# Half of the triangular inversions done 16 wide and merged by two small products, with a product and the mixture moved

## The chip, the cores and the metric

The kernel runs on one core of one Trainium2 chip. The time is the device time of one execution in microseconds (us); lower is better. TensorE is called PE in the profile (its weight loads PEld), VectorE DVE, ScalarE ACT, GpSimd POOL, and SyncE (which issues nearly all DMAs here) SP.

## The reference

A recurrence over 768 time steps runs for 4 batches of 8 heads with a 40 by 40 state, and its output goes through a gated mixture over the sequence:

```
for t in range(S):
    y[:, :, t] = einsum('bhd,bhde->bhe', r_t, state)
    Sa = einsum('bhde,bhe->bhd', state, a_t)
    state = state * w_t[:, :, None, :] - einsum('bhd,bhe->bhde', Sa, b_t) + einsum('bhd,bhe->bhde', v_t, k_t)
x = y, heads side by side                      # 768 x 320 for each batch
h = maximum(x @ w_in, 0); u, v = halves of h   # 512 columns each
v = (v - mean) / sqrt(var + 1e-6)              # over the 512 columns
v = einsum('ts,bsd->btd', w_spatial, v) + b_spatial[:, None]
out = (u * v) @ w_out
```

## The kernel before, in words

**The recurrence in chunks.** `phase1` cuts the time axis into chunks of 64 steps. Two batches are worked on together, so there are 24 chunk steps, numbered 0 to 23 below, 12 for each pair of batches. In a chunk the steps are solved at once by a lower triangular system with unit diagonal. Its inverse is needed. Each 64 by 64 triangle is cut into blocks of 32: the two diagonal blocks are inverted on DVE, and the block below them is made of products (`b_l21`, `b_zt`, `b_x21`).

**The inversion.** `lprime` (PE) and `lblock` (DVE) make the diagonal blocks of one chunk, tile `Lc`. For four chunks, a group, `invert` transposes them into `A` (DVE), does 30 substitution steps of two DVE instructions each (lines 351 and 355), and transposes the result into `XT0` and `X11` (lines 360 and 362). It runs as a generator: one step at a time is put among the other DVE work. Group 0 is done in one go at the start, since chunk 0 waits for it. Groups 1 to 5 are for chunks 4 to 7, 8 to 11 and so on.

**The step.** For chunk s, and two halves g of the heads, `c_bp` (PE) multiplies the carried state `Mc`, `c_bp_out` (ACT) evicts it, `c_ff` and `c_ff_out`, `c_xx` and `c_xx_out` follow in the same way, `c_mp` and `c_mp_out` (DVE, tiles `mn` and `Mc`) make the next state, `c_y` and `c_y_out` (DVE, tile `y`) the output. The products of chunk s+1 that don't need the state (`b_copy`, `b_lka`, `b_lka_out`, `b_tok`, `b_h` and so on) and the preparation of later chunks (`scan1`, `scan2`, `at_mul`, `sl_mul` on DVE) stand between them. `b_lka` is the masked product: its result is evicted by ACT into `At` and masked there by POOL (`strict`).

**The order.** Each function is put into a list with a time, `at(t, fn, ...)`, in units of chunk steps; the list is sorted, and the instructions of each engine stand in that order and run in it. The small products of phase 1 write tiles named `bk` from a pool of two PSUM buffers, so a product waits until the one two before it has been read.

**The mixture.** `decode` (DVE, ACT, POOL) turns `w_in` into two float32r parts, from step `T_DEC` on. The mixture's first product (`m_u`, four of each six slots, and `m_v`, two of six) has 72 slots, four for each chunk step, from step `T_MOE` on. What is left of them after chunk 23 runs in between the instructions of `phase2` (`spatial`, lines 173 to 178, and `proj`, line 193), which a scheduler puts in order. The loads of phase 2 for a batch, `vload`, take memory that the mixture's tiles hold until they are done.

## Time and profile before

| What | Value |
|---|---|
| Runs | 725.81 us median of 3 (721.95 to 728.2) |
| The profiled execution | 728.03 us, its span 726.2 us |
| Mean granted clock of TensorE | 0.901 |
| Busy share: PE, PEld, DVE, ACT, POOL | 82%, 74%, 62%, 57%, 40% |
| Chunk steps 0 to 22 | 29.8 to 524.9 us of the span |
| From chunk step 23 to the end | 524.9 to 726.2 us |

The busy shares are means over a span with three different parts: the start, the chunk steps without the mixture (0 to 10) and those with it (11 to 22), and the end, where phase 2 takes over. What bounds the time is read for each part by itself, by cutting the span at the first product of each `c_bp`.

### The profile page before, as it was taken

Reading aid. Unit: us, or ns where it says so; the run is one execution under the profiler, and the core shown is the slowest. Engines: PE = TensorE matmul, PEld = TensorE weight load, DVE = VectorE, ACT = ScalarE, POOL = GpSimd, SP = SyncE. Lnnn points to the kernel's source line nnn. Section 1 sums busy time; section 2 is a strip of 40 time slices with the busy share of each in tenths; the row PEclk is TensorE's granted clock in tenths of the full one; section 3 lists DMA queues with packets and bytes.
Section 4 is the critical chain, followed back from the end, with each engine's and each line's share of the span. In section 5 each row is a group of like instructions: output and inputs, shape, how many; then the busy total and the mean of one; then the engine's idle time right before and its main releaser. Section 6 shows DMA issues by size and latency. Waiting matters only on the chain. (4 is left out here: it accounts for less than half of the span.)

```text
span 726.2 us, 25447 instructions
## 1 busy us (share of the span) xinstructions
PE 592.8 (82%) x10784; PEld 535.0 (74%) x10784; DVE 448.6 (62%) x884; ACT 415.1 (57%) x904; POOL 289.7 (40%) x486
## 2 busy tenths in 40 slices
PE   2707776587776877989988999899999999599997
PEld 1606665586665776868877788788789998499997
DVE  7898689968999998758797565311247201343221
ACT  2406763377655666878878798798754423332112
POOL 4102230124433435354554543464549822373221
PEclk9956997578977888989999999999899999799999
DMA  9443675294444535454365344344263533650001
GB/s 186 86 90 69 104 145 112 51 185 94 106 91 101 112 82 118 112 126 112 102 187 165 85 133 127 106 120 116 73 198 108 158 108 100 189 180 34 28 28 55
DMA packets 101337, 81.35 MB, mean 112 GB/s; under 512 B 33576, under 2 KB 90152, under 8 KB 99304
## 3 DMA queue, kind: packets, MB, share of 16 engines
q1 hardware_dynamic: 100680, 78.01, 43.3%
q10 hardware_dynamic: 544, 1.72, 1.1%
q8 instruction: 85, 1.39, 0.9%
q14 instruction: 28, 0.23, 0.1%
HBM read 59.20 MB, written 20.50 MB: 110 GB/s over the span
## 5 line engine op out<-in xcount | busy, mean ns | idle before, releaser
L396 POOL TENSOR_SCALAR_AFFINE_SELECT Rt<-Rt 64x512 f32<-64x512 f32 (+1 forms) x144 | 84.1, 585 | 102.2 <-ACT Rt L582 74.4
L545 ACT ACTIVATE Rt<-bp 64x416 f32<-64x416 f32 x96 | 49.1, 512 | 68.2 <-PE bp L535 66.4
L351 DVE TENSOR_TENSOR itmp<-A 128x30 f32<-128x30 f32 (+9 forms) x180 | 73.7, 409 | 3.3
L396 POOL TENSOR_SCALAR_AFFINE_SELECT At<-At 64x512 f32<-64x512 f32 x48 | 36.9, 768 | 94.6 <-ACT At L406 92.5
L173 PE MATMUL pg<-wsh,vh 128*128 128x384 f32 x192 | 65.1, 339 | 0.0
L174 PE MATMUL pg<-wsl,vh 128*128 128x384 f32 x192 | 65.0, 339 | 0.0
L175 PE MATMUL pg<-wsh,vl 128*128 128x384 f32 x192 | 64.8, 337 | 0.0
L355 DVE TENSOR_TENSOR A<-A,itmp 128x30 f32<-128x30 f32 (+9 forms) x180 | 59.0, 328 | 6.2
L535 PE MATMUL bp<-lin,Mc 40*64 40x104 f32 x768 | 53.1, 301 | 11.1 <-DVE y L640 10.3
L535 PEld LDWEIGHTS bp<-lin,Mc 40*64 40x64 f32 x768 | 46.2, 167 | 16.0 <-DVE y L640 13.4
L177 DVE TENSOR_TENSOR g<-pg,bb 128x384 f32<-128x384 f32 x32 | 17.7, 553 | 63.9 <-PE pg L175 56.9
L702 DVE BATCH_NORM_STATS2 bs<-vr 128x6 f32<-128x512 f32 x24 | 16.6, 690 | 60.3 <-ACT vr L696 60.2
L54 POOL TENSOR_TENSOR gl<-g,gh 128x384 fp32r<-128x384 f32 x32 | 33.8, 1062 | 47.7 <-ACT gh L50 47.7
L582 ACT ACTIVATE Rt<-ch 64x416 f32<-64x416 f32 x96 | 49.2, 512 | 3.9 <-PE ch L571 1.5
L326 PE MATMUL bk<-at,sl 64*32 64x32 f32 x1536 | 24.4, 221 | 28.6 <-DVE sl L313 14.5
L553 PE MATMUL ch<-Rt,At 128*64 128x104 f32 x768 | 46.0, 277 | 1.2 <-issue 1.2
L50 ACT ACTIVATE gh<-g 128x384 fp32r<-128x384 f32 x32 | 16.7, 522 | 52.3 <-DVE g L178 52.3
L441 PE MATMUL bk<-ident,sl 128*128 128x128 f32 x192 | 31.7, 297 | 17.4 <-ACT tk L447 6.9
L553 PEld LDWEIGHTS ch<-Rt,At 128*64 128x64 f32 x768 | 40.3, 152 | 5.7 <-issue 3.0
L326 PEld LDWEIGHTS bk<-at,sl 64*32 64x32 f32 x1536 | 20.6, 132 | 30.7 <-DVE sl L313 14.6
L571 PE MATMUL ch<-ffs,xf 64*64 64x104 f32 x768 | 42.6, 263 | 0.0
L54 POOL TENSOR_TENSOR vl<-raw,vh 128x512 fp32r<-128x512 f32 x24 | 32.1, 1350 | 25.8 <-ACT vh L50 24.8
(121 smaller groups left out, 1604.2 us busy)
## 6 DMA issues: line engine op xcount, KB each, us to landing
ein<-in_early SPq DMA_DIRECT2D x40, 387.0 KB
lin<-in_late SPq DMA_DIRECT2D x48, 160.0 KB
uts<-ur SPq DMA_DIRECT2D x48, 128.0 KB
vns<-vr SPq DMA_DIRECT2D x24, 256.0 KB
raw<-vns SPq DMA_DIRECT2D x24, 256.0 KB
ut<-uts SPq DMA_DIRECT2D x24, 256.0 KB
Rt<-in_vtok SPq DMA_DIRECT2D x48, 80.0 KB
xs<-y SPq DMA_DIRECT2D x48, 80.0 KB
```

The lines of the kernel that those rows point to most:

```text
L54: eng.tensor_tensor(out=lo, in0=x, in1=hi.bitcast(F32), op=ALU.subtract)
L173: nc.tensor.matmul(pg, lhsT=vh[:, dc], rhs=w_h, start=(i == 0), stop=False)
L174: nc.tensor.matmul(pg, lhsT=vh[:, dc], rhs=w_l, start=False, stop=False)
L175: nc.tensor.matmul(pg, lhsT=vl[:, dc], rhs=w_h, start=False, stop=(i == NT - 1))
L326: nc.tensor.matmul(pl[o:o + HB, n, :], lhsT=sl[PR[par], n, par, cs], rhs=at[PR[par], n, cs], start=True, stop=True,)
L351: nc.vector.tensor_tensor(out=tp, in0=A[:, k + 1:, k:k + 1].broadcast_to([P, m, k]), in1=A[:, k:k + 1, 0:k].broadcast_to([P, m, k]), op=AL ...
L355: nc.vector.tensor_tensor(out=A[:, k + 1:, 0:k], in0=A[:, k + 1:, 0:k], in1=tp, op=ALU.add)
L396: nc.gpsimd.affine_select(out=t, in_=t, pattern=[[0, k], [1, C]], base=0, channel_multiplier=-1, compare_op=ALU.is_gt, fill=0.0,)
L535: nc.tensor.matmul(bp[PR[par], q, :], lhsT=Mc[RR[par], n, :], rhs=li[RR[par], n, C:], start=(q == 0), stop=False, skip_group_check=True,)
L545: nc.scalar.activation(Rt[par][PR[par], gp, :], st["bp", g][PR[par]], AF.Copy)
L553: nc.tensor.matmul(ff[PR[1 - par], q, :], lhsT=At[par][:, n, :], rhs=Rt[par][:, n, :], start=True, stop=True,)
L582: nc.scalar.activation(Rt[par][PR[par], gp], xx[PR[1 - par]], AF.Copy, scale=-1.0)
```

## The change

Four things are done. Groups 1 and 2 (chunks 4 to 11) are inverted by `invert16`: the two 16 wide diagonal blocks of each 32 wide block are inverted together, in 14 steps of two DVE instructions on both at once, after a second memset; the block below them comes from two products on PE for each chunk (`merge_z`, `merge_x`) with an ACT eviction between them and a DVE addition and a DVE transpose behind them. `Lc` gets three buffers. `b_copy`, `b_lka` and `b_lka_out` go behind `c_ff`, so that `At` needs one buffer for the chunk it serves, and `b_tok` comes to where they were. `T_DEC` goes from 4.2 to 3.2 and `T_MOE` from 11 to 10. `b_h_out` of chunk 0 is written ahead of the first inversion, which leaves its engines' order as it was.

```diff
+    QB = 16
+    QUAD = (1, 2)
...
-            st["Lc", s // GS] = inv.tile([P, GS * NU, HB], F32, name="Lc")
+            st["Lc", s // GS] = inv.tile([P, GS * NU, HB], F32, name="Lc", bufs=3)
...
+    def invert16(g):
+        Lc = st["Lc", g]
+        Af = inv.tile([P, HB * HB + HB], F32, name="A")
+        A = Af[:, 0:HB * HB].rearrange("p (t s) -> p t s", s=HB)
+        D = Af.rearrange("p (b x) -> p b x", b=2)[:, :, 0:HB * QB]
+        D = D.rearrange("p b (t s) -> p b t s", s=HB)[:, :, :, 0:QB]
+        nc.vector.transpose(out=A, in_=Lc.rearrange("p u t -> p t u"))
+        yield
+        nc.vector.memset(Af[:, 0:HB * HB:HB + 1], 1.0)
+        nc.vector.memset(A[:, QB:, 0:QB], 0.0)
+        for k in range(1, QB - 1):
+            m = QB - 1 - k
+            tp = ps_i.tile([P, 2, m, k], F32, name="itmp")
+            nc.vector.tensor_tensor(
+                out=tp, in0=D[:, :, k + 1:, k:k + 1].broadcast_to([P, 2, m, k]),
+                in1=D[:, :, k:k + 1, 0:k].broadcast_to([P, 2, m, k]), op=ALU.mult,
+            )
+            nc.vector.tensor_tensor(
+                out=D[:, :, k + 1:, 0:k], in0=D[:, :, k + 1:, 0:k], in1=tp, op=ALU.add
+            )
+            yield
...
+        nc.vector.transpose(out=X11.rearrange("p u t -> p t u"), in_=A.rearrange("p t s -> p s t"))
+        yield
+        nc.vector.transpose(out=XT0.rearrange("p u t -> p t u"), in_=A)
+        yield
+
+    def merge_z(s):
...
+        zp = ps_k.tile([P, NU, HB], F32, name="bk")
+        for n in range(NU):
+            for o in range(0, P, HB):
+                nc.tensor.matmul(
+                    zp[o:o + HB, n, :], lhsT=Lc[o:o + QB, u0 + n, :],
+                    rhs=X11[o:o + QB, u0 + n, :], start=True, stop=True,
+                )
+        z = Lc[:, u0:u0 + NU]
+        nc.scalar.activation(z, zp, AF.Copy)
...
+    def merge_x(s):
...
+        xp = ps_k.tile([P, NU, QB], F32, name="bk")
+        for n in range(NU):
+            for o in range(0, P, HB):
+                nc.tensor.matmul(
+                    xp[o:o + HB, n, :], lhsT=z[o:o + HB, n, :],
+                    rhs=XT0[o:o + HB, u0 + n, QB:], start=True, stop=True,
+                )
+        nc.vector.tensor_tensor(out=XT0[:, us, QB:], in0=xp, in1=XT0[:, us, QB:], op=ALU.add)
+        nc.vector.transpose(
+            out=X11[:, us].rearrange("p u t -> p (u t)"), in_=XT0[:, us].rearrange("p u t -> p (u t)")
+        )
...
-            at(b + 0.11 + 0.02 * par, b_copy, q, par)
-            at(b + 0.17 + 0.02 * par, b_lka_out, q, par)
+            at(b + 0.38 + 0.01 * par, b_copy, q, par)
+            at(b + 0.44 + 0.01 * par, b_lka_out, q, par)
...
-            at(b + 0.40 + 0.03 * par, b_tok, q, par)
-            at(b + 0.43 + 0.03 * par, b_tok_out, q, par)
-        at(b + 0.115, b_lka, q)
+            at(b + 0.12 + 0.03 * par, b_tok, q, par)
+            at(b + 0.14 + 0.03 * par, b_tok_out, q, par)
+        at(b + 0.40, b_lka, q)
...
+        b = GS * g - 1
+        if g in QUAD:
+            gen = invert16(g)
+            for k in range(QB - 1):
+                at(t0 + (b - 0.1 - t0) * k / (QB - 2), step, gen)
+            at(b + 0.02, step, gen)
+            at(b + 0.10, step, gen)
+            for j in range(GS):
+                at(b + j + 0.26, merge_z, GS * g + j)
+                at(b + j + 0.47, merge_x, GS * g + j)
+            continue
...
-    T_DEC, T_MOE = 4.2, 11
+    T_DEC, T_MOE = 3.2, 10
```

The order shows the change at three places. The first is DVE in chunk step 3, from the `y` of chunk 2 to the next state; there before stand 50 rows from `Lc` to the first `mn`, of which these are the first three and the last ten:

```order
L337 TENSOR_TENSOR Lc<-bk,maskl 128x256
L351 TENSOR_TENSOR itmp<-A 128x238
L355 TENSOR_TENSOR A<-A,itmp 128x17x14
...
L355 TENSOR_TENSOR A<-A,itmp 128x2x29
L351 TENSOR_TENSOR itmp<-A 128x30
L355 TENSOR_TENSOR A<-A,itmp 128x30
L281 SCALAR_TENSOR_TENSOR S<-ein_121,ends 128x528
L285 RECIPROCAL ends<-S 128x8
L360 STREAM_TRANSPOSE XT_1890<-A 128x32x32
L362 STREAM_TRANSPOSE X_1891<-A 128x32x32
L290 SCALAR_TENSOR_TENSOR Et<-ein_121,ends 128x528
L307 TENSOR_TENSOR at<-ein_121,Et 128x512
```

And now 20 rows stand there, of which these are the first twelve and one more (lines 396 and 398 are the transposes of `invert16`, 64 is the decoding, 428 is `merge_x`):

```order
L339 TENSOR_TENSOR Lc<-bk,maskl 128x256
L396 STREAM_TRANSPOSE X_1668<-A 128x32x32
L398 STREAM_TRANSPOSE XT_1667<-A 128x32x32
L283 SCALAR_TENSOR_TENSOR S<-ein_120,ends 128x528
L287 RECIPROCAL ends<-S 128x8
L292 SCALAR_TENSOR_TENSOR Et<-ein_120,ends 128x528
L309 TENSOR_TENSOR at<-ein_120,Et 128x512
L64 TENSOR_SCALAR d_t_1756<-d_raw 128x512
L315 TENSOR_TENSOR sl<-ein_120,S 128x1024
L339 TENSOR_TENSOR Lc<-bk,maskl 128x256
L69 TENSOR_SCALAR d_t_1757<-d_raw 128x512
L428 TENSOR_TENSOR XT_1667<-bk,XT_1667 128x8x16
```

The substitution has left chunk step 3 altogether (it ends in step 2), and the decoding and the merge have come in.

The second place is PE in chunk step 6, from `c_bp` to `c_xx`. Before, `b_lka` (line 389) stands between `c_bp` (535) and `c_ff` (553), and `b_tok` (441) and `b_l21` (458) between `c_ff` and `c_xx` (571):

```order
L535 MATMUL bp_2728<-lin_136,Mc 64x104 x8
L535 MATMUL bp_2746<-lin_136,Mc 64x104 x8
L389 MATMUL bk<-at,sl 64x64 x16
L553 MATMUL ch<-Rt_132,At_2424 64x104
...
L441 MATMUL bk<-ident,sl 128x128 x8
L458 MATMUL bk<-sl,at 32x32 x16
L571 MATMUL ch<-ffs,xf_130 64x104 x16
```

Now `b_tok` (508) and `merge_z` (408) stand ahead of `c_ff` (621), and `b_lka` (453) and `merge_x` (424) behind it:

```order
L602 MATMUL bp_2886<-lin_136,Mc 64x104 x8
L602 MATMUL bp_2904<-lin_136,Mc 64x104 x8
L508 MATMUL bk<-ident,sl 128x128 x8
L408 MATMUL bk<-X_1668,Lc 32x32 x32
L621 MATMUL ch<-Rt_132,At_2619 64x104
...
L453 MATMUL bk<-at,sl 64x64 x16
L424 MATMUL bk<-XT_1667,Lc 32x16 x32
L525 MATMUL bk<-sl,at 32x32 x16
L639 MATMUL ch<-ffs,xf_130 64x104 x16
```

The masked product and the transposes of `b_tok` have changed places, and 64 small matmuls have come in.

The third is ACT in chunk step 0, behind the evictions of `c_bp`. Before, the copies into `At` (382) and the evictions of `b_lka` (406) stand ahead of the eviction `sc` of the scan (299), and the `tk` (447) behind it:

```order
L382 ACTIVATE At_606<-at 64x512
L382 ACTIVATE At_607<-at 64x512
L406 ACTIVATE At_606<-bk 64x512
L406 ACTIVATE At_607<-bk 64x512
L299 ACTIVATE sc<-S 128x8
L561 ACTIVATE ffs<-ch 128x416 x2
L447 ACTIVATE tk<-bk 128x320
L486 ACTIVATE zt<-bk 32x256 x2
L756 ACTIVATE xf_130<-XT_557 128x8x32
L756 ACTIVATE xf_130<-XT_557 32x8x32 x2
L447 ACTIVATE tk<-bk 128x320
L513 ACTIVATE xf_130<-bk 32x8x32 x2
```

Now (lines 514, 301, 629, 446, 553, 470, 824 and 580 for the same):

```order
L514 ACTIVATE tk<-bk 128x320 x2
L301 ACTIVATE sc<-S 128x8
L629 ACTIVATE ffs<-ch 128x416
L446 ACTIVATE At_654<-at 64x512
L629 ACTIVATE ffs<-ch 128x416
L446 ACTIVATE At_655<-at 64x512
L553 ACTIVATE zt<-bk 32x256 x2
L470 ACTIVATE At_654<-bk 64x512
L824 ACTIVATE xf_130<-XT_561 128x8x32
L824 ACTIVATE xf_130<-XT_561 32x8x32 x2
L470 ACTIVATE At_655<-bk 64x512
L580 ACTIVATE xf_130<-bk 32x8x32 x2
```

Four evictions of `At` have moved from ahead of `sc` to behind it, and two of `tk` the other way. In the later chunk steps the same instructions change places in the same way.

## Rows read from the trace of the kernel before

**Rows 1.** Windows cut at each first `c_bp`: length, busy times, granted clock, DMA.

```profile
core 0: us, PE busy (x) PEld busy (x) DVE busy (x) ACT busy (x) POOL busy (x), PEclk, DMA share, GB/s
...
92.24:114.08 21.84, 15.15 (x465) 13.37 (x457) 19.68 (x40) 12.89 (x29) 5.77 (x8) 0.92 0.75 151
114.08:143.90 29.82, 17.38 (x426) 15.45 (x426) 28.48 (x61) 12.26 (x27) 4.52 (x8) 0.68 0.36 69
143.90:165.30 21.40, 17.97 (x490) 16.19 (x490) 13.80 (x30) 13.42 (x29) 5.04 (x8) 0.74 0.79 163
165.30:184.80 19.50, 14.53 (x393) 13.04 (x392) 18.89 (x36) 13.05 (x29) 8.58 (x10) 0.89 0.38 88
...
246.40:266.40 20.00, 15.08 (x398) 13.59 (x394) 19.53 (x36) 12.93 (x29) 8.42 (x10) 0.84 0.30 62
266.40:287.20 20.80, 15.84 (x393) 14.06 (x394) 18.51 (x33) 13.78 (x30) 10.56 (x12) 0.83 0.60 126
...
409.30:427.00 17.70, 16.92 (x360) 14.79 (x360) 12.00 (x31) 16.21 (x36) 6.33 (x16) 1.00 0.39 119
```

**Rows 2.** Waits of PE in 143 to 287 us: us, times, longest.

```profile
PE bk L326 <- issue: 11.3, 5, 3.2
PE bp L535 <- DVE y L640: 6.5, 4, 3.4
PE bk L441 <- ACT At L406: 5.3, 6, 1.2
```

**Rows 3.** Waits of PE in 305 to 525 us, the longest in total.

```profile
PE ch L603 <- ACT Rt L582: 6.2, 10, 1.1
```

**Rows 4.** Timeline of DVE, group 0's inversion: start, us, instruction.

```profile
28.98 1.95 DVE L345 STREAM_TRANSPOSE A<-Lc 128x1024 f32<-128x1024 f32 x1
31.01 0.20 DVE L351 TENSOR_TENSOR itmp<-A 128x30 f32<-128x30 f32 x1
...
38.92 0.40 DVE L351 TENSOR_TENSOR itmp<-A 128x228 f32<-128x228 f32 x1
...
51.31 0.28 DVE L351 TENSOR_TENSOR itmp<-A 128x108 f32<-128x108 f32 x1
...
51.92 0.26 DVE L351 TENSOR_TENSOR itmp<-A 128x84 f32<-128x84 f32 x1
...
53.00 0.20 DVE L351 TENSOR_TENSOR itmp<-A 128x30 f32<-128x30 f32 x1
...
53.45 1.91 DVE L360 STREAM_TRANSPOSE XT<-A 128x1024 f32<-128x1024 f32 x1
```

**Rows 5.** Timeline of PE in chunk step 2.

```profile
97.69 0.76 PE L326 MATMUL bk<-at,sl 64*32 64x32 f32 x64
```

**Rows 6.** Timeline of ACT in chunk step 0.

```profile
34.02 1.27 ACT L382 ACTIVATE At<-at 64x512 f32<-64x512 f32 x2
35.19 1.19 ACT L406 ACTIVATE At<-bk 64x512 f32<-64x512 f32 x2
58.31 0.21 ACT L299 ACTIVATE sc<-S 128x8 f32<-128x8 f32 x1 [21.92 <-DVE S L281]
...
64.70 1.05 ACT L582 ACTIVATE Rt<-ch 64x416 f32<-64x416 f32 x2
```

**Rows 7.** The page's DMA queues: packets, MB, share.

```profile
q8 instruction: 85, 1.39, 0.9%
```

**Rows 8.** The chain that ended last, in order of time: one slot of each kind.

```profile
607.68 0.95 PE pv L739 x8
...
609.68 1.87 PE pv L694 x8
```

**Rows 9.** Waits of PE from 525 us to the end: us, times, longest.

```profile
PE po L193 <- ACT gh L50: 7.2, 1, 7.2
```

**Rows 10.** Windows in the part from chunk step 23 on, columns as in rows 1.

```profile
605.00:625.00 20.00, 15.63 (x86) 12.69 (x84) 2.32 (x7) 6.05 (x13) 4.09 (x15) 1.00 0.30 99
625.00:645.00 20.00, 13.72 (x69) 13.72 (x70) 10.38 (x17) 6.75 (x13) 13.20 (x17) 0.74 0.55 158
```

More of the change, by code (lines that the diff above doesn't have):

```diff
@@ L343, in invert @@
         Lc = st.pop(("Lc", g))
-        A = inv.tile([P, HB, HB], F32, name="A")
+        A = inv.tile([P, HB * HB + HB], F32, name="A")[:, 0:HB * HB]
+        A = A.rearrange("p (t s) -> p t s", s=HB)
         nc.vector.transpose(out=A, in_=Lc.rearrange("p u t -> p t u"))
@@ L365, in phase1 @@
     INV_N = HB + 1
+    def invert16(g):
[19 more added lines that the diff above has]
+            yield
+        XT0 = xinv.tile([P, GS * NU, HB], F32, name="XT0")
+        X11 = xinv.tile([P, GS * NU, HB], F32, name="X11")
+        st["X", g] = (XT0, X11)
+        nc.vector.transpose(out=X11.rearrange("p u t -> p t u"), in_=A.rearrange("p t s -> p s t"))
+        yield
+        nc.vector.transpose(out=XT0.rearrange("p u t -> p t u"), in_=A)
+        yield
@@ new lines, in merge_z @@
+    def merge_z(s):
+        XT0, X11 = st["X", s // GS]
+        Lc = st["Lc", s // GS]
+        u0 = (s % GS) * NU
+        zp = ps_k.tile([P, NU, HB], F32, name="bk")
[7 more added lines that the diff above has]
+        nc.scalar.activation(z, zp, AF.Copy)
+        st["z", s] = z
@@ new lines, in merge_x @@
+    def merge_x(s):
+        XT0, X11 = st["X", s // GS]
+        u0 = (s % GS) * NU
+        us = slice(u0, u0 + NU)
+        z = st.pop(("z", s))
+        xp = ps_k.tile([P, NU, QB], F32, name="bk")
[9 more added lines that the diff above has]
+        )
@@ L377, in b_copy @@
         if par == 0:
-            At = [jat.tile([P, NU, C], F32, name=f"At{i}") for i in range(2)]
-            tk = jit.tile([P, NU, 2, E], F32, name="tk")
-            st["blk", s] = (At, Rts[s % 2], tk, xfs[s % 2])
+            st["At"] = [jat.tile([P, NU, C], F32, name=f"At{i}", bufs=1) for i in range(2)]
         at = st["pre", s][1]
-        nc.scalar.activation(st["blk", s][0][par][PR[par]], at[PR[par]], AF.Copy)
+        nc.scalar.activation(st["At"][par][PR[par]], at[PR[par]], AF.Copy)
     def b_lka(s):
@@ L401, in b_lka_out @@
     def b_lka_out(s, par):
-        At = st["blk", s][0]
+        At = st["At"]
         pk = st["pk", s]
@@ L437, in b_tok @@
     def b_tok(s, h):
+        if h == 0:
+            tk = jit.tile([P, NU, 2, E], F32, name="tk")
+            st["blk", s] = (Rts[s % 2], tk, xfs[s % 2])
         sl = st["pre", s][2]
@@ L447, in b_tok_out @@
         nc.scalar.activation(
-            st["blk", s][2][:, h * NP:(h + 1) * NP],
+            st["blk", s][1][:, h * NP:(h + 1) * NP],
             st.pop(("pt", s, h)).rearrange("p n (h e) -> p n h e", h=2)[:, :, :, 0:E], AF.Copy,
@@ L542, in c_bp_out @@
         gp, ns = grp(g)
-        Rt = st["blk", s][1]
+        Rt = st["blk", s][0]
         for par in range(2):
@@ L548, in c_ff @@
         gp, ns = grp(g)
-        At, Rt, tk, xf = st["blk", s]
+        Rt, tk, xf = st["blk", s]
+        At = st["At"]
         ff = ps_c.tile([P, NP, NR], F32, name="ch")
@@ L565, in c_xx @@
         gp, ns = grp(g)
-        xf = st["blk", s][3]
+        xf = st["blk", s][2]
         ffs = st["ffs", g]
@@ L577, in c_xx_out @@
         gp, ns = grp(g)
-        Rt = st["blk", s][1]
+        Rt = st["blk", s][0]
         xx = st["xx", g]
@@ L598, in c_mp @@
         gp, ns = grp(g)
-        At, Rt, tk, xf = st["blk", s]
+        Rt, tk, xf = st["blk", s]
         mp = st["xx", g][:, :, C:]
@@ L622, in c_y @@
         gp, ns = grp(g)
-        At, Rt, tk, xf = st["blk", s]
+        Rt, tk, xf = st["blk", s]
         bp = st["bp", g]
@@ L814, in phase1 @@
         t0 = 2.5 if g == 1 else max(4.5, GS * g - 4 + 0.0)
-        t1 = GS * g - 1 + 0.70
+        b = GS * g - 1
[9 more added lines that the diff above has]
+            continue
         gen = invert(g)
         for k in range(INV_N):
-            at(t0 + (t1 - t0) * k / (INV_N - 1), step, gen)
-    T_DEC, T_MOE = 4.2, 11
+            at(t0 + (b + 0.70 - t0) * k / (INV_N - 1), step, gen)
+    T_DEC, T_MOE = 3.2, 10
     for i in range(6):
@@ L916, in phase1 @@
         b_h(0)
-        for _ in invert(0):
-            pass
         b_h_out(0, 0)
         b_h_out(0, 1)
+        for _ in (invert16(0) if 0 in QUAD else invert(0)):
+            pass
+        if 0 in QUAD:
+            merge_z(0)
+            merge_x(0)
+            for j in range(1, GS):
+                at(j - 1 + 0.46, merge_z, j)
+                at(j - 1 + 0.56, merge_x, j)
         open_fifo()
```

## Prediction

> **What bounds the kernel now.** I first cut the span at the first carry product of each chunk step, since the busy shares of the whole mix parts with different limits. The reader should compare DVE's busy time with the length of each window [rows 1]. In chunk step 3 DVE is busy for 28.48 of 29.82 us, in step 5 for 18.89 of 19.50, in step 9 for 19.53 of 20.00: steps 3 and 5 to 10 are bound by DVE. Step 4 is not (13.80 of 21.40); there PE is busy for 17.97 us at a granted clock of 0.74. With the mixture (step 17) PE is busy for 16.92 of 17.70 us and ACT for 16.21: both are nearly full, DVE is not.
>
> Next the waits of PE in steps 4 to 10 [rows 2]. The wait for `y` is DVE's lateness at the end of a step. But more, 11.3 us in five waits, is put down to "issue", that is, to nothing that the profile shows. One queue of the page carries 85 packets of kind "instruction", 1.39 MB, some 16 KB each [rows 7]; that these waits are for such packets is my reading, no row ties them together. In the mixture's steps PE waits for little, and for ACT [rows 3].
>
> Last the part behind step 22. PE's only long wait there is one of 7.2 us [rows 9]. It stands behind the mixture's last slots, which run alone from 605 us on, with PE busy for 15.63 of 20 us; behind the wait PE works at half the clock for a while (1.2 of 2.4 GHz; 0.74 over that window) [rows 10].
>
> **The change part by part.** Times are for the profiled execution, 728.03 us, which is 2.2 us over the median of the runs; plus is a saving.
>
> *DVE work.* Group 0 shows what 32 wide substitution costs: from 31.01 to 53.45 us, 22.4 us [rows 4]. The new one has 14 pairs of 28 to 112 elements. A pair of 30 takes 0.45 us there (53.00 to 53.45), one of 108 takes 0.61 (51.31 to 51.92); so 14 pairs cost between 6.3 and 8.7 us, and by size 7.8. The second memset, of 256 elements, lies between the 0.20 us of 30 elements and the 0.40 of 228: 0.3. Each merge adds an addition of 128 elements (0.28 us for 108, 0.40 for 228: 0.3) and a transpose of 128x256: a quarter of the 1.95 us of one four times as large is 0.5, the upper end is that 1.95 itself; I take 0.6, since the other instructions scale with size in the rows. A group then costs 7.8 + 0.3 + 4 x 0.9 = 11.7 us (9 to 18) in the place of 22.4.
>
> *Steps 2 and 3.* Group 1's substitution used to be spread from the middle of step 2 to the end of step 3. Eleven of its 30 pairs stood ahead of step 2's last `y` (7.9 us, 31.01 to 38.92 in group 0), nineteen behind it (14.5 us). Now all 14 and the memset lie ahead, 8.1 us, and 13 of them ahead of the first `y`, some 0.5 us more, on the engine that sets that step. **-0.7.** Step 3 loses the 14.5 us and gets the merge (0.9) and five decoding instructions (of 512 elements, taken as 0.65 us each, 3.3 in all). 29.8 - 14.5 + 4.2 = 19.5 by DVE alone. The merge now waits for PE and ACT in between, with the scan of chunk 11 queued behind its addition, and PE has 17.38 + 1.4 and its own waits: 20.8. **+9.0** (7 to 10).
>
> *Step 4.* Not DVE bound; it gains nothing from DVE and gets the merges. 64 small matmuls take 0.76 us in `lprime` [rows 5]; two products with 64 each are 1.4 us, and at most 2.2 with the half clock. Against that stands a better clock, since step 3 leaves PE less idle. **0** (-2 to +2).
>
> *Steps 5 to 9.* From 165.3 to 266.4 us they take 20.2 us each. DVE falls to 16.2 us in steps 5 to 7: a group's 22.4 and three transposes (5.8) over 3.7 steps are 7.6 us a step, 8.1 and 5.8 over 3.6 are 3.9, and the merge is 0.9, so 18.9 - 7.6 + 4.8. What is late next is PE: 14.8 us busy, 1.4 for the merges, 1.6 for issue (11.3 over seven steps), and the waits for `bk` buffers. Of those the one of `b_tok` for `At` (5.3 in six) goes, since `b_tok` now stands ahead; but `merge_z` waits for the eviction of `tk`, and `b_l21` behind `merge_x` for that of `At`: some 0.8 us more than before, with `c_ff` and `c_xx` queued behind them on PE. 18.6 us; steps 5 to 7 give **+5.0** (0 to 9). Step 8 has decoding and the 32 wide inversion of group 3 as before, and the merge on top: **-0.3**. Step 9 has lost its decoding and is bound by PE: **+1.5**.
>
> *Step 10.* DVE gives way, but four slots of the mixture come in: 3 x 0.95 + 1.87 = 4.7 us at the full clock [rows 8], 5.5 with their share of the ends. PE has 15.84 + 1.4 + 5.5 less what the better clock gives back (some 2.5): 20.3. **+0.3.**
>
> *Step 0.* ACT waits until 58.31 us for `sc`, that is, for the first scan behind the inversion, and `c_xx`'s eviction starts at 64.70 [rows 6]. The moved copies and evictions of `At` (1.27 + 1.19 us) used to lie ahead of that wait, at no cost; now they lie behind it, in the queue ahead of the evictions that `c_xx` waits for. Two evictions of `tk` (0.9) go the other way. 1.6 us, and more where `b_x21` waits for the `bk` buffer that the second `At` eviction reads. **-3.0** (-1.6 to -3.5).
>
> *Steps 11 to 22.* The work is the same. On ACT the copies and evictions of `At` now stand behind `c_ff` instead of filling the time in which PE makes it, so ACT has some 0.9 us without work at the front and that much more to do ahead of `c_xx`'s evictions; PE has some 1 us of other products there to cover it. Against this, the mixture's slots are shifted by one step, so the decoding of `w_out` in step 15 no longer meets the same slots. **-1.0** (-13 to +4).
>
> *The end.* Four slots fewer are left behind step 22: 5.5 us of a stretch where PE is full, and two of the seven that run alone, each with some 0.6 us of waiting. The 7.2 us behind the last slot stay, since the loads of the second batch wait for the mixture's memory as before. **+6.7** (4 to 10).
>
> Sum: -3.0 - 0.7 + 9.0 + 0 + 5.0 - 0.3 + 1.5 + 0.3 - 1.0 + 6.7 = 17.5. 728.03 - 17.5 = 710.5; less the 2.2 by which this execution lies over the median, 708.3. I forecast 708.
>
> **The rivals.**
>
> *PE takes DVE's place completely.* Each merge brings 128 matmuls where a step has 390, so the issue waits, 1.6 us in a step, may grow more than in proportion, and such waits come with the half clock, as in steps 4 to 10 (0.74 to 0.89) [rows 1]. For it: step 4, with 490 matmuls and DVE idle, took 21.4 us. Steps 5 to 9 then stay at 20 us and step 4 grows by 2: 708 + 5.5 + 2 = 715.5. Against it: half of step 4 went by at the half clock (0.74), behind the idle time that step 3 leaves on PE.
>
> *The issue waits are hidden.* If PE spends none in steps 4 to 9, those without another bound come to 17 us, 1.6 less for five steps, and step 4 gains 2: 708 - 8 - 2 = 698. For it: the mixture's steps have hardly any such wait. Against it: 11.3 us of them [rows 2] before PE gets a third more instructions in these steps. The Trainium skill (Runtime: NRT & Kernel Launch, Instruction fetch mechanics) says that an engine's instructions are refilled in 16 KiB blocks while it works through others, and that this is mostly hidden; by that rule this rival is the forecast. The trace's 11.3 us put down to issue speak against it, if my reading of them is right.
>
> *ACT becomes the bound with the mixture (slower).* The place is `c_mp` in steps 10 to 22, which already waits for ACT ten times in twelve steps [rows 3]. If the 0.9 us of ACT's idle time isn't covered and the following stretch also falls to the half clock (as at 625 to 645 us behind a wait), a step costs 2 us more: 13 x 2 = 26, and 708 + 26 = 734. The kernel is slower from 1.4 us a step on. Against it: PE has 7 to 8 us of products between `c_ff` and `c_mp`, about what ACT needs there, and the clock stayed at 1.00 in step 17 in spite of such waits.
>
> *The mixture's shift gives nothing.* If the end waits for the same loads at the same distance, or step 10 grows by what the end loses: 708 + 7 = 715.
>
> **How the numbers follow.** Forecast 0.45 (701 to 714 by its own bounds), PE in DVE's place 0.20, issue hidden 0.18, no gain from the shift 0.11, ACT 0.06. The range leaves out the ACT case and a little on each side: 695 to 720. A difference under 1% (718.6 to 733.1) can't be told from none here. Faster by more: the forecast, the hidden issue and most of the two cases around 715, 0.83; the same 0.12; slower 0.05.
>
> **What would show it.** In the profile after: step 3 at some 21 us with DVE still nearly full; steps 5 to 7 at 18 to 19 us with PE, not DVE, nearly full and `c_bp` no longer waiting for `y`; `c_xx`'s first eviction in step 0 at 66 us or later; `c_bp` of step 23 some 10 us earlier than 524.9; from there to the end some 195 us in the place of 201; the one wait of 7 us behind the mixture still there. I am wrong if step 3 stays over 25 us (the merge's chain through PE and ACT then holds DVE), if steps 11 to 22 grow by more than 1 us each, or if the end doesn't shrink.

## The result, and the profile after

The changed kernel takes 728.87 us (median of 20 runs, 725.13 to 738.22), the kernel before 725.29 beside it (20 runs). The ratio is 1.005, 95% interval 1.0026 to 1.0073: half a per cent slower, within the 1% called no change, where 708 us, and so a faster kernel, was forecast. Two of the gains came as predicted, on DVE in step 3 and at the end. They were given back elsewhere.

Line numbers behind the diff are higher: `c_bp` L602, `c_mp` L671, `c_xx`'s evictions L650, the evictions of the masked product `b_lka` L470, of `tk` L514, the merges L408 and L424. These are windows of the changed kernel, cut at first `c_bp` as in [rows 1]: steps 3, 4 and 5, then steps 0 to 10, 11 to 22 and the end.

```profile
core 0: us, PE busy (x) PEld busy (x) DVE busy (x) ACT busy (x) POOL busy (x), PEclk, DMA share, GB/s
115.02:136.00 20.98, 17.73 (x553) 16.09 (x553) 19.53 (x30) 12.84 (x28) 7.10 (x8) 0.80 0.53 101
136.00:163.69 27.69, 18.11 (x619) 16.00 (x617) 16.02 (x31) 14.33 (x31) 7.88 (x10) 0.82 0.60 122
163.69:182.57 18.88, 15.51 (x522) 14.02 (x521) 16.48 (x34) 13.66 (x30) 8.29 (x10) 0.91 0.40 97
29.42:283.69 254.27, 186.85 (x5700) 167.88 (x5696) 205.45 (x397) 153.57 (x340) 83.97 (x105) 0.84 0.52 109
283.69:536.54 252.85, 231.74 (x4635) 201.62 (x4627) 138.29 (x308) 201.14 (x431) 116.36 (x234) 0.93 0.44 118
536.54:725.80 189.26, 174.83 (x1135) 169.36 (x1134) 55.82 (x105) 60.70 (x125) 80.46 (x119) 0.98 0.34 105
```

The same three parts of the kernel before, in the same columns:

```profile
29.83:287.19 257.36, 175.85 (x4644) 157.50 (x4642) 227.69 (x441) 147.25 (x327) 80.50 (x104) 0.79 0.52 106
287.19:524.95 237.76, 220.13 (x4617) 190.55 (x4609) 135.06 (x299) 195.44 (x427) 111.99 (x223) 0.95 0.45 120
524.95:726.10 201.15, 186.01 (x1184) 177.66 (x1184) 62.53 (x114) 64.49 (x134) 86.62 (x131) 0.97 0.34 107
```

Step 3 fell from 29.82 to 20.98 us and step 5 from 19.50 to 18.88, as the DVE account said: DVE's busy time in steps 0 to 10 fell by 22 us. But PE's rose by 11, some 4.7 of it the mixture's first slots in step 10 [rows 8]; step 4 grew from 21.40 to 27.69, and all eleven steps together gained only 3. Steps 11 to 22 grew by 15.1 us, of which 3.1 are eighteen products of the spatial part that used to lie behind the start of step 23. The end shrank by 11.9, these 3.1 among them.

Waits of PE in steps 4 to 10, then in steps 11 to 22, against [rows 2, 3]: us, times, longest.

```profile
PE bk L525 <- ACT At L470: 5.9, 6, 1.8
PE ch L639 <- issue: 4.6, 1, 4.6
PE bk L408 <- ACT tk L514: 4.0, 4, 1.0
...
PE bk L328 <- issue: 2.6, 3, 1.2
PE bk L453 <- issue: 2.5, 1, 2.5
```

```profile
PE ch L671 <- ACT Rt L650: 8.4, 11, 1.2
PE bk L508 <- ACT tk L514: 3.7, 3, 2.2
PE pv L807 <- ACT ur L809: 3.1, 2, 2.0
```

DVE's `y` has left the first list. What stands in its place are ACT's evictions. The waits for "issue" fell in all, from 15.9 to 12.0 us, but 8.3 of them now lie in step 4, where the kernel before had one:

```profile
PE bk L326 <- issue: 1.6, 1, 1.6
```

In the second list the wait of `c_mp` has grown from 6.2 to 8.4 us only. The transposes of `b_tok`, which waited 2.7 us for other evictions, now wait 3.7 for a buffer that `tk`'s eviction frees, and the mixture's products wait 3.1 us for ACT, where they waited 0.3.

The timeline of PE in step 4, the instructions behind a wait for "issue":

```profile
146.01 1.15 PE L453 MATMUL bk<-at,sl 64*64 64x64 f32 x31 [2.48 <-issue]
154.52 3.04 PE L639 MATMUL ch<-ffs,xf 64*64 64x104 f32 x31 [4.64 <-issue]
163.54 0.21 PE L328 MATMUL bk<-at,sl 64*32 64x32 f32 x1 [1.14 <-issue]
```

The three are 8.3 us. The step grew by 6.3. ACT in step 0, against [rows 6]:

```profile
57.88 0.21 ACT L301 ACTIVATE sc<-S 128x8 f32<-128x8 f32 x1 [23.10 <-DVE S L283]
58.40 0.61 ACT L446 ACTIVATE At<-at 64x512 f32<-64x512 f32 x1
...
62.49 0.59 ACT L470 ACTIVATE At<-bk 64x512 f32<-64x512 f32 x1
65.83 1.05 ACT L650 ACTIVATE Rt<-ch 64x416 f32<-64x416 f32 x2
```

All four `At` instructions now stand behind `sc`, and `c_xx`'s eviction starts at 65.83 in the place of 64.70. The wait behind the mixture stayed, 8.1 us against 7.2 [rows 9]:

```profile
PE po L193 <- ACT gh L50: 8.1, 1, 8.1
```

### The profile page after: what moved, and what is told of

Read it like the earlier page. It is cut to its first block, busy times and chain, and to the rows that moved or that the text cites. A ratio compares the mean times of both kernels' runs of the same rounds, so it can differ in the third digit from the quotient of the medians.

```text
span 725.9 us, 27425 instructions
## 1 busy us (share of the span) xinstructions
PE 604.3 (83%) x11808; PEld 548.2 (76%) x11808; DVE 422.9 (58%) x838; ACT 423.4 (58%) x912; POOL 291.4 (40%) x486
## 5 line engine op out<-in xcount | busy, mean ns | idle before, releaser
L650 ACT ACTIVATE Rt<-ch 64x416 f32<-64x416 f32 x96 | 49.0, 511 | 10.2 <-PE ch L639 7.7
L639 PE MATMUL ch<-ffs,xf 64*64 64x104 f32 x768 | 45.2, 272 | 5.9 <-issue 5.9
L602 PE MATMUL bp<-lin,Mc 40*64 40x104 f32 x768 | 44.5, 270 | 6.8 <-DVE y L708 5.5
L684 DVE TENSOR_TENSOR mn<-ch,Mc 104x160 f32<-104x160 f32 x44 | 14.1, 321 | 59.7 <-PE ch L671 43.4
L354 DVE TENSOR_TENSOR itmp<-A 128x30 f32<-128x30 f32 (+14 forms) x120 | 45.2, 377 | 2.4
L602 PEld LDWEIGHTS bp<-lin,Mc 40*64 40x64 f32 x768 | 39.2, 146 | 8.8 <-DVE y L708 5.8
L639 PEld LDWEIGHTS ch<-ffs,xf 64*64 64x64 f32 x768 | 39.5, 146 | 7.7 <-issue 6.6
L770 DVE BATCH_NORM_STATS2 bs<-vr 128x6 f32<-128x512 f32 x24 | 16.5, 687 | 48.5 <-ACT vr L764 48.5
L621 PE MATMUL ch<-Rt,At 128*64 128x104 f32 x768 | 42.9, 267 | 0.0
L358 DVE TENSOR_TENSOR A<-A,itmp 128x30 f32<-128x30 f32 (+14 forms) x120 | 39.4, 328 | 4.1
L621 PEld LDWEIGHTS ch<-Rt,At 128*64 128x64 f32 x768 | 37.8, 145 | 4.1 <-issue 2.3
L544 PE MATMUL bk<-XT,l 32*32 32x32 f32 x768 | 19.2, 197 | 24.9 <-DVE XT L363 17.8
L54 POOL TENSOR_TENSOR vl<-raw,vh 128x512 fp32r<-128x512 f32 x24 | 31.3, 1311 | 21.0 <-ACT vh L50 13.2
```

The source lines that it names most:

```text
L54: eng.tensor_tensor(out=lo, in0=x, in1=hi.bitcast(F32), op=ALU.subtract)
L354: nc.vector.tensor_tensor(out=tp, in0=A[:, k + 1:, k:k + 1].broadcast_to([P, m, k]), in1=A[:, k:k + 1, 0:k].broadcast_to([P, m, k]), op=AL ...
L602: nc.tensor.matmul(bp[PR[par], q, :], lhsT=Mc[RR[par], n, :], rhs=li[RR[par], n, C:], start=(q == 0), stop=False, skip_group_check=True,)
L621: nc.tensor.matmul(ff[PR[1 - par], q, :], lhsT=At[par][:, n, :], rhs=Rt[par][:, n, :], start=True, stop=True,)
L639: nc.tensor.matmul(xx[ev, q, :], lhsT=xf[ev, n, :], rhs=ffs[ev, q, :], start=True, stop=True,)
L650: nc.scalar.activation(Rt[par][PR[par], gp], xx[PR[1 - par]], AF.Copy, scale=-1.0)
```

## The experiments

The change has three parts: the 16-wide inversion of chunks 4 to 11, the move (`b_tok` ahead; `b_copy`, `b_lka` and its evictions behind `c_ff`; one `At` buffer) and the shift (mixture a step earlier). The expectations name these theories. A: the move delays ACT ahead of `c_mp` in steps 11 to 22. B: the merges fill PE in steps 4 to 10, the move is neutral. C: the shift makes steps 11 to 22 slower. D: PE's own order or the single buffer, not ACT's load. E: the single `At` buffer. F: the merges cost more than steps 5 to 7 gain. G: `c_bp` loses its neighbour on PE. M and N: the merges cost much, or little. Ratios are against the kernel before on the same chip. Stretches and waits are those of one profiled execution, which lies up to 9 us off the median of its kernel's runs.

**The parts one by one.** Without the move `At` has two buffers again, and then the third `Lc` buffer doesn't fit; where the inversion runs without the move, `Lc` has two, and `lprime` of chunks 12, 13, 16 and 17 comes late, behind the merges that free a buffer.

The edits, against the changed kernel: first without the inversion, then without the move, then without the shift.

```diff
-    QUAD = (1, 2)
+    QUAD = ()
```

```diff
-            at(b + 0.38 + 0.01 * par, b_copy, q, par)
-            at(b + 0.44 + 0.01 * par, b_lka_out, q, par)
+            at(b + 0.11 + 0.02 * par, b_copy, q, par)
+            at(b + 0.17 + 0.02 * par, b_lka_out, q, par)
...
-            at(b + 0.12 + 0.03 * par, b_tok, q, par)
+            at(b + 0.40 + 0.03 * par, b_tok, q, par)
...
```

```diff
-    T_DEC, T_MOE = 3.2, 10
+    T_DEC, T_MOE = 4.2, 11
```

Move alone: 

> The kernel before with the masked product moved behind c_ff alone (At single, b_tok in its place); all inversions 32 wide, mixture from step 11. Theory A, the move delays the evictions ahead of c_mp on ACT and so costs the changed kernel some 10 us in steps 11 to 22: 734 to 740 us, with PE waiting some 1 us at c_mp in most of these steps. Theory B, the merges fill PE in steps 4 to 10 and the move is neutral: 724 to 728. Theory C, the earlier mixture makes steps 11 to 22 slower: also 724 to 728.

Shift alone: 

> The kernel before with decoding and mixture one step earlier alone. Theory A: 716 to 720 us (four mixture slots leave the end, steps 11 to 22 stay). Theory B: the same. Theory C: 726 to 732, with steps 11 to 22 longer by some 10 us.

Move and shift: 

> The changed kernel with all inversions 32 wide and unmerged: the move and the shift without the merges. Theory A: 727 to 733 us, the loss of the move against the gain of the shift, so the inversion itself is worth little more than nothing. Theory B: 716 to 720, the merges are what costs. Theory C: 726 to 732.

Inversion and shift, no move: 

> The changed kernel with the masked product where it was before and At double; to fit the memory Lc has two buffers, and lprime of chunks 12, 13, 16 and 17 comes later in its step or one to two steps later. Theory A: 712 to 718 us, steps 11 to 22 as before the change and step 0 as before. Theory B: 726 to 731, as the changed kernel. Theory C: 725 to 731.

Inversion alone: 

> The 16-wide inversion alone: no move, mixture as before. With the earlier mixture the inversion changed 717.3 to 719.4, that is by +0.1 to +0.3%. If it adds to the mixture's gain in the same way: 724 to 728 (ratio 0.998 to 1.004). If the early mixture takes the idle time that the inversion would have freed (theory C in part), it gains by itself: 712 to 719.

| parts | median us | ratio, 95% interval | steps 0-10 | 11-22 | end |
|---|---|---|---|---|---|
| none (before, profiled once) | 725.8 | 1 | 257.4 | 237.8 | 201.2 |
| all three | 728.9 | 1.0050 (1.0026 to 1.0073) | 254.3 | 252.8 | 189.3 |
| move | 743.8 | 1.0297 (1.0241 to 1.0354) | 256.5 | 252.7 | 204.2 |
| shift | 717.3 | 0.9929 (0.9895 to 0.9964) | 262.3 | 233.2 | 190.2 |
| inversion | 734.0 | 1.0111 (1.0070 to 1.0151) | 261.2 | 232.4 | 200.3 |
| move and shift | 734.2 | 1.0179 (1.0128 to 1.0230) | 257.7 | 250.4 | 193.5 |
| inversion and shift | 719.4 | 0.9940 (0.9899 to 0.9981) | 268.3 | 231.8 | 189.3 |

The shift pays, with 11 us at the end. Whether it also shortens steps 11 to 22 isn't shown: the inversion alone, without the shift, has 232.4 us there, and the time that TensorE spent at 1.2 GHz in these steps differs with the execution (25.6 us in the kernel before, 13.7 and 3.4 in two executions of the shift alone). The move costs 2.5 to 3%: with it steps 11 to 22 take 250 us and more, without it 232 to 238, whatever else is there. C falls, and of B the half that calls the move neutral. The inversion adds nothing to the shift (717.3 and 719.4), though step 3 falls by 10 us there too. Alone it costs 1.1%, 734.0 us, which neither expectation had; where is open, since the execution that was profiled took 725.02 us, among the fastest of its runs.

**What of the move costs.** The shift alone runs at 233.2 us in steps 11 to 22, with the move at 250.4. PE's waits there, first without, then with the move:

```profile
PE ch L671 <- ACT Rt L650: 6.4, 9, 1.1
...
PE bk L508 <- ACT xf L580: 1.4, 2, 1.1
```

```profile
PE ch L671 <- ACT Rt L650: 9.9, 12, 1.2
PE bk L508 <- ACT tk L514: 4.4, 3, 2.2
```

Of the 17.2 us, waits of over 0.15 us are 7.4 (14.8 to 22.2, added up from the trace), and the stretches at 1.2 GHz grow from 13.7 to 23.9 us, which is 5.1 lost if half of such a stretch is (an estimate). The rest is on PE itself. The timeline of PE at the start of step 13, without the move:

```profile
328.77 1.38 PE L602 MATMUL bp<-lin,Mc 40*64 40x104 f32 x26
329.90 0.27 PE L453 MATMUL bk<-at,sl 64*64 64x64 f32 x2
329.98 0.26 PE L602 MATMUL bp<-lin,Mc 40*64 40x104 f32 x2
330.01 0.28 PE L453 MATMUL bk<-at,sl 64*64 64x64 f32 x3
...
330.18 0.87 PE L453 MATMUL bk<-at,sl 64*64 64x64 f32 x24
330.98 0.62 PE L807 MATMUL pv<-xh,wh 128*128 128x256 f32 x3
```

and with it:

```profile
326.50 1.64 PE L602 MATMUL bp<-lin,Mc 40*64 40x104 f32 x32
328.07 1.09 PE L508 MATMUL bk<-ident,sl 128*128 128x128 f32 x8
...
331.62 1.15 PE L453 MATMUL bk<-at,sl 64*64 64x64 f32 x32
332.70 0.62 PE L807 MATMUL pv<-xh,wh 128*128 128x256 f32 x3
```

Where the masked product follows `c_bp`, the two run into one another, and both are done 2.21 us after the start (328.77 to 330.98). Apart they take 1.57 and 1.08, 2.65 in all: 0.44 us more in this step. Among themselves `c_bp`'s products are no faster: two start every 89 ns in both kernels. But in the first the trace has the first eight masked products start among the last six of `c_bp`, though the program puts them behind all 32; in the second 180 ns pass from `c_bp`'s last product to the transposes. The mean time from a `c_bp` product to PE's next product, whichever it is, at the full clock in steps 11 to 22, is 39 to 41 ns in before and in the shift alone, and 50 or 51 in all kernels in which the move, or a half of it, holds there. The program puts the two on different quarters: `c_bp` reads half `par` of the partitions and writes half `par`, the masked product reads half `par` and writes the other. The Trainium skill (TensorE: Matmul & The Clock Gate, Part 3: Packing small matmuls) says that products on separate parts of the array run at the same time; this trace agrees, and shows it for products of two different steps of a program, here 40*64 beside 64*64.

Then four kernels on what in the move does this. DVE in the place of ACT and POOL for the masked product's eviction, in the changed kernel:

```diff
-    H_POOL, LKA_POOL, TRI_POOL = range(0, 99), range(0, 99), range(0, 99)
+    H_POOL, LKA_POOL, TRI_POOL = range(0, 99), range(0, 11), range(0, 99)
```

> The changed kernel with one thing altered: from chunk 11 on the masked product's result is evicted by DVE with a multiplication by the mask, not by ACT with a copy and a mask on POOL, so that ACT has two instructions of about 0.6 us less in each of steps 10 to 22, in the place to which the move brought them. Theory A (the moved evictions stand on ACT ahead of the eviction that the c_mp products wait for): steps 11 to 22 fall from 252.8 us by 8 to 16, the kernel comes to 713 to 721. Theory D (the move costs by the order of TensorE's own instructions or by the single At buffer, ACT's load matters little): no change, 726 to 731.

721.59 us, 0.9956 (0.9923 to 0.9989), steps 11 to 22 at 241.7, 11 less: as A said, if slightly less in the whole. But the profiled execution, at 717.08 us, was the fastest, and most of the 11 us isn't in waits: those of over 0.15 us fell only from 20.7 to 18.4 us, and the time at 1.2 GHz from 34.1 to 13.7. The same in the kernel with move and shift:

> The move and the earlier mixture without the 16-wide inversion (734.2), with the masked product evicted by DVE from chunk 11 on. Theory A: steps 11 to 22 fall from 250.4 by 8 to 12 us as in the changed kernel (252.8 to 241.7) and the kernel to 722 to 726; what is left over the earlier mixture alone is c_bp's 5 us and waits for the token evictions. If the gain there came from other things: 731 to 736.

726.51 us, 1.0062 (1.0018 to 1.0105), against 1.0179 without the edit: the same edit brings 1.2% here and 0.9% in the changed kernel. Steps 11 to 22 are at 244.9 us in the profiled execution (730.77 us), 5.5 less where 8 to 12 were expected; here the time at 1.2 GHz is 23.9 us with and without the edit, and the waits fell by some 4 (22.2 to 18.1). So ACT's queue is part of what the move costs. Two `At` buffers (`bufs=1` taken away, `st["At", s]` for `st["At"]`) with move and shift:

> The move and the earlier mixture without the 16-wide inversion (734 when run before), but with At in two buffers again: the copies and the masked product keep their late place, and no longer share the buffer that c_ff has just read. Theory A (the place in the order costs): no change, 731 to 737. Theory E (the single buffer costs, since the copy into At must wait until c_ff has read it): back to the earlier mixture alone, 716 to 721.

729.31 us, 1.0069 (1.0034 to 1.0104), steps 11 to 22 at 246.1. Neither end: the single buffer is worth some 1.1% of the 2.5, which A had put at nothing. Then the two halves of the order, with the shift. The late half (`b_tok` back at 0.40, one `At` buffer):

> The move in half, with the earlier mixture and without the 16-wide inversion: the copies into At, the masked product and its evictions stand late (0.38 to 0.45 of a step), the token transposes stay where they were before (0.40 to 0.46). Whole move 734, no move 717. If the late evictions alone cost (theory A), 730 to 737; if the token transposes early in the step cost, whose evictions then stand between those of c_bp and those of c_ff, 716 to 722; half each about 726.

and the early half (`b_tok` behind `c_bp`, the rest in its early place, two `At` buffers):

```diff
-            at(b + 0.40 + 0.03 * par, b_tok, q, par)
-            at(b + 0.43 + 0.03 * par, b_tok_out, q, par)
+            at(b + 0.101 + 0.002 * par, b_tok, q, par)
+            at(b + 0.102 + 0.002 * par, b_tok_out, q, par)
```

> The earlier mixture, no 16-wide inversion, and of the move only this: the token transposes come right behind c_bp, ahead of the masked product, and their evictions behind those of c_bp; the copies and the masked product keep their early place behind them. Theory G (c_bp's products lose by having no small products of the masked product right behind them, 0.4 us in each of 23 steps, and ACT has the token evictions early): 725 to 732, c_bp at 50 ns a product in steps 11 to 22. Theory A alone (what costs are the copies and evictions of the masked product that stand late): 715 to 721.

742.46 us, 1.0235 (1.0186 to 1.0284), and 738.45, 1.0238 (1.0165 to 1.0311). Both are slower than every range expected for them. Each half costs at least as much as the whole (3.1% against 2.5), so they don't add up, and the halves can't be used as a split. Steps 11 to 22 show why; the waits of PE there, of the late half and of the early one:

```profile
PE bk L508 <- ACT tk L514: 12.7, 12, 2.8
PE ch L671 <- ACT Rt L650: 5.1, 9, 1.1
```

```profile
PE bk L453 <- ACT tk L514: 13.9, 12, 2.4
PE ch L671 <- ACT Rt L650: 5.5, 8, 1.1
```

Transposes and masked product now stand side by side, each wants `bk` buffers, and PE waits once in every step until ACT has evicted `tk`; `c_bp` is at 50 ns in both. G had the price of `c_bp` right (3.7 us in twelve steps) and not this wait. Against theory A, `c_mp` waits less here than with the whole move, and the kernel is as slow.

**ACT's load without the move.** The first kernel is the shift alone with the masked product evicted by DVE from chunk 11 on; it was run again beside the shift alone, and then two more evictions followed.

> The control of the run with DVE's eviction: the earlier mixture alone (717.3, no move, no 16-wide inversion), and from chunk 11 on the masked product evicted by DVE. If ACT's load is only a trouble where the move has put it (theory A), this gains little on 717.3: 714 to 719. If ACT's load bounds steps 11 to 22 wherever it stands, it gains the same 7 to 8 us as with the move: 708 to 711.

> The earlier mixture alone once more (717.3, ratio 0.9929 on another chip), beside the next kernel on one chip. Theory A: ratio 0.99 to 0.996 again. If chips differ for the same kernel: 0.980 to 0.985.

> The earlier mixture with DVE's eviction from chunk 11 on once more (707.5, ratio 0.9805). Its profile differed from that of the earlier mixture alone by 1.4 us in steps 11 to 22 and by 7.4 in steps 0 to 10, where the two have the same instructions. If that was a difference of chips or of executions: within 0.5% of the kernel beside it here. If DVE's eviction is worth it by itself: 0.978 to 0.984, with the gain in steps 11 to 22.

With two evictions on DVE, and with three:

```diff
-    H_POOL, LKA_POOL, TRI_POOL = range(0, 99), range(0, 11), range(0, 99)
+    H_POOL, LKA_POOL, TRI_POOL = range(0, 99), range(0, 11), range(0, 11)
```

```diff
-    H_POOL, LKA_POOL, TRI_POOL = range(0, 99), range(0, 11), range(0, 99)
+    H_POOL, LKA_POOL, TRI_POOL = range(0, 11), range(0, 11), range(0, 11)
```

> The earlier mixture, DVE's eviction of the masked product from chunk 11 on (709.7, 226.5 us in steps 11 to 22), and from chunk 11 on also c_xx's masked half evicted by DVE, so that ACT's eviction ahead of c_mp is half as wide. If ACT ahead of c_mp is what steps 11 to 22 still wait for: the wait of c_mp for it falls from 6.7 us to under 3, the steps by 4 to 10, the kernel to 700 to 706. If TensorE's own order and time bound them: 707 to 712.

> The same with the third masked eviction (b_h's) on DVE too from chunk 11 on: ACT has six instructions less in a step than with the earlier mixture alone. If ACT's load bounds the steps: another 2 to 5 us, 697 to 704; if not, as the kernel beside it within 2 us; if DVE is then late for y: 710 to 716.

One eviction: 707.50 us, 0.9805 (0.9759 to 0.9852), and again 709.67, 0.9852 (0.9774 to 0.9930). The shift alone again: 714.57, 0.9894 (0.9852 to 0.9936). Both medians lie at the range that the first expectation gave for a bound by ACT's load wherever it stands. But on one chip the two are 0.4% apart by their ratios, with intervals that overlap (4.9 us by their medians), within the 0.5% named for a difference of chips or executions, and in the first pair 7 of the 9 us lay in steps 0 to 10, where the kernels are the same up to step 10. So how much the edit gives without the move isn't settled; steps 11 to 22 lost 1.4 us in one pair and 5.4 in the other. The wait of `c_mp` for ACT didn't fall: 6.4 and 8.6 us in the first pair, 6.7 and 6.7 in the second. The version is the fastest of all that were run, but for the one that leaves out the merges (below), which lies beside it. Two evictions: 727.08 us, 1.0068 (1.0033 to 1.0102); three: 736.82, 1.0186 (1.0149 to 1.0223). With two, PE waits for DVE at the same place:

```profile
PE ch L671 <- DVE Rt L658: 13.6, 13, 3.6
PE bp L602 <- DVE y L708: 4.6, 4, 1.9
```

Taking more from ACT made the steps slower, since `c_mp` now waits for DVE (13.6 us with two). So these two don't test whether ACT's load bounds the steps without the move: they put another engine in its place. It stays open.

**The move where DVE is late, and nowhere else.** All parts, with two `At` and two `Lc` buffers and the late `lprime`:

```diff
+    LAST_MOVED = 11
...
-            at(b + 0.38 + 0.01 * par, b_copy, q, par)
+            at(b + (0.38 + 0.01 * par if mv else 0.11 + 0.02 * par), b_copy, q, par)
```

> All three parts, but the move only for chunks 1 to 11 (steps 0 to 10, in which DVE is late), with At in two buffers and Lc in two; from chunk 12 on the copies, the masked product and the transposes stand where they stood before. Theory A: steps 0 to 10 as in the changed kernel (254), steps 11 to 22 as with the earlier mixture alone (232 to 234), the end 189: 704 to 711, faster than both kernels and than every run so far. If the move costs as much in steps 0 to 10 as the inversion gives there: 715 to 720.

722.83 us, 0.9956 (0.9914 to 0.9999). Steps 0 to 10, then 11 to 22:

```profile
29.39:295.15 265.76, 204.31 (x5700) 183.98 (x5696) 206.21 (x397) 154.69 (x340) 81.67 (x106) 0.76 0.50 105
295.15:526.15 231.00, 215.78 (x4629) 187.36 (x4621) 137.54 (x303) 196.99 (x430) 118.82 (x233) 0.98 0.46 129
```

The second row is what A asked: 252.85 falls to 231.00 with the move undone in these steps alone. The first row isn't: 11.5 us over the changed kernel, at a granted clock of 0.76 against 0.84. What differs there are the buffers and the late `lprime`; steps 6 and 10, where it comes, take 25.2 and 27.0 us (18.3 and 19.9 in the changed kernel), as in the kernel without any move (24.3 and 25.7). That the third `Lc` buffer is worth this much is argued from these steps, not tested: two `At` and three `Lc` buffers don't fit.

**The merges.** Chunks 4 to 7 alone with the new inversion, with the shift and without the move (`QUAD = (1,)`, two `Lc` buffers, `lprime` of chunks 12 and 13 late):

> No move; earlier mixture; only chunks 4 to 7 inverted by 16-wide substitution and products, chunks 8 to 11 by 32-wide substitution. The earlier mixture alone ran at 717.3 and with both groups at 719.4. If the merges' products cost more in steps 4 to 10 than the shorter substitution gives in steps 5 to 7, and step 3 alone gains (theory F), this is the fastest: 708 to 713. If the gain of step 3 is given back in step 4 by the merges of its own group whatever follows, 715 to 720.

718.48 us, 0.9929 (0.9894 to 0.9964): the same ratio as the shift alone. F falls; step 3 is 9.8 us shorter than there, and steps 4 to 6 are 9.3 longer, 2.9 of them in step 6, where the late `lprime` of chunk 12 comes. Then the changed kernel without the merges:

```diff
-                at(b + j + 0.26, merge_z, GS * g + j)
-                at(b + j + 0.47, merge_x, GS * g + j)
+                pass
```

> The changed kernel without the two products and their evictions that complete the 16-wide inverses of chunks 4 to 11 (the lower left 16 x 16 part of each 32 x 32 block is left out of the inverse): 1,024 matmuls, 8 ACT and 16 DVE instructions less. Theory M (the merges' 13.2 us of matmuls, and the instruction blocks and waits that come with them, take back what the short substitution frees): steps 4 to 10 fall from 147.7 by 13 to 20 us and the kernel to 709 to 716. Theory N (TensorE has room for them, another wait sets steps 4 to 10): steps 4 to 10 fall by less than 6, the kernel to 723 to 729. Of the waits of TensorE for its own instructions: if these come with the count of instructions, they come every 127 to 128 matmuls here too, and none at the instant at which the changed kernel has its 4.64 us.

709.48 us, 0.9831 (0.9786 to 0.9876). Steps 4 to 10 fall from 147.7 to 134.5 us, here in one window:

```profile
133.59:268.07 134.48, 113.02 (x2873) 101.20 (x2873) 115.47 (x210) 96.32 (x209) 60.89 (x72) 0.84 0.52 118
```

M holds, at its lower end: 13.2 us in these steps and 1.8 in step 3, 15.0 where the merges lie (the span fell by 18.3, the rest of it in steps without merges). The merges' own matmuls are busy for 13.2 us in the changed kernel, on all eight chunks. In step 4, now 22.08 us long, waits for "issue" of 5.1 us are left, at other instructions:

```profile
PE bk L571 <- issue: 4.0, 1, 4.0
...
PE ch L639 <- issue: 1.1, 1, 1.1
```

## Why the prediction was wrong

Term by term, profiled execution against profiled execution, plus is a saving:

| term | predicted | measured |
|---|---|---|
| step 0 | -3.0 | -4.1 (step 1 gives 2.4 back) |
| step 2 | -0.7 | +0.3 |
| step 3 | +9.0 | +8.8 |
| step 4 | 0 | -6.3 |
| steps 5 to 7 | +5.0 | +5.0 |
| step 8 | -0.3 | -2.4 |
| step 9 | +1.5 | -1.7 |
| step 10 | +0.3 | +1.0 |
| steps 11 to 22 | -1.0 | -15.1 |
| end | +6.7 | +11.9 |

**The step that failed is "Steps 11 to 22", with its opening "The work is the same".** It is 14 of the 17 us that are missing from the 17.5 forecast. The prediction followed the moved instructions on ACT alone, 0.9 us that other products would cover, and put the loss at 1.0 us, with -13 as its bound. Its own sign of being wrong, more than 1 us a step there, came. Undoing the move in these steps brought 22 us back (the time at 1.2 GHz fell with it, from 34.1 to 10.2), so the place in the program is shown; but the wait of `c_mp`, 2.2 us more than before, is the small part. What the step did not look at is what the moved products leave behind on PE: `c_bp` lost the neighbour that ran beside it, 3.6 us more in twelve steps here. The transposes wait for `bk` buffers behind ACT's queue (3.7 us, 1.0 more) and the mixture's products for ACT (3.1, 2.8 more), while others went, so that the waits of over 0.15 us, that of `c_mp` among them, grew by 4.2 us in all, from 16.5 to 20.7. The time at 1.2 GHz grew from 25.6 to 34.1 us, which is 4.3 if half of such a stretch is lost. With the 3.1 us of spatial products that makes 15.2, for 15.1 measured. This sum is an estimate, and that it comes out so closely is luck in part: a wait or a `c_bp` product at 1.2 GHz is counted twice. The rival "ACT becomes the bound with the mixture", at 0.06 and 2 us a step, had the sign, the place and the order of size (1.0 us a step without the spatial products), but of its mechanism the wait of `c_mp` is 2.2 of the 12 us and the half clock some 4.3. That DVE's eviction took some 4 us of waits from steps 11 to 22 of the kernel with move and shift, at the same time at 1.2 GHz, shows that ACT's queue is part of the cause; that it is all of it isn't shown.

**"Step 4", 0 (-2 to +2), failed too**, and with it steps 8 and 9. The merges were priced by the duration of `lprime`, 1.4 us each [rows 5], and their matmuls took about that, 13.2 us for eight. The whole price was 15 us in steps 3 to 10, against 11.2 (8 x 1.4) in the terms, and it fell where there was no room: without the merges step 4 is at 22.08 us. In steps 4 to 10 the merges also bring waits of PE for ACT (4.0 us in four waits for `tk` ahead of `merge_z`), and the waits for "issue" there are 12.0 us with them, 7.1 without; in step 4 these are 8.3, against 5.1 without the merges and 1.6 in the kernel before. The term for step 4 had no price for either. The rival "PE takes DVE's place completely" said so for step 4, with 2 us in the place of 6.3. It was wrong on steps 5 to 7, which took 18.9, 18.3 and 19.2 us against 18.6 predicted. That agreement is luck in part: the mark named with it, PE nearly full, did not come (busy for 15.5, 15.6 and 14.7 us, DVE for 16.5, 15.6 and 17.4).

**What held.** DVE's account was right: step 3 at 20.98 us (20.8 predicted), with DVE busy for 19.53 of it. Step 0 had its mechanism, and `c_xx`'s eviction at 65.83 us (66 or later was named). Step 10's term is a slip of 0.2 in the working, 20.8 less 20.3; nothing hangs on it. The end gained 8.8 us without the 3.1, against 6.7, and the long wait behind the mixture stayed; "The mixture's shift gives nothing" is refuted by the shift alone. "The issue waits are hidden" was refuted by step 4 alone.

**Left open:** why the packet behind a wait for "issue" (last section) at times comes late; how the move's 17 us divide between buffers, order and clock, since its halves don't add up; and what the inversion would give with room for both buffers.

## What to carry to other kernels

When an instruction is moved, look at the place that it leaves as well: which products ran beside it on TensorE, and which buffers turned round in that gap. An engine that is relieved by products on another gains only what the other has to spare, waits included: 22 us off DVE's busy time left 3 us in steps 0 to 10, where the mixture's first slots had come in as well. Try the parts of a change alone: one of these three, the earlier mixture, was worth 0.7 to 1.1% and was hidden by the move.
